# A Fourier mixing and gated convolution kernel: DFT tables laid out by quarter, odd products ahead of the halved rows, three memsets in the set-up

## The chip, the cores and the metric

The kernel runs on one core of one Trainium2 chip. The metric is the device time of one execution in microseconds (us), as a median over runs. The core's engines appear in the profile as PE (TensorE, matrix products; PEld are its weight loads), DVE (VectorE), ACT (ScalarE), POOL (GpSimd) and SP (SyncE, which here only issues DMAs). Each engine works through its own instructions in the order in which the program gives them to it; between engines, and between an engine and a DMA, the framework that builds the program puts in waits wherever two instructions touch the same data.

## What is computed

The reference, cut to what matters. The input `x` is 8 x 3136 x 256, `w_in` 256 x 1024, `conv_w` 3 x 1024, `w_out` 1024 x 256, all float32:

```python
X = np.fft.fft(x, axis=1)
X = np.fft.fft(X, axis=2)
x = X.real.astype(np.float32)

h = np.maximum(x @ w_in, 0.0)
hp = zero-padded h, one row at each end of the sequence
conv_out = sum over k of conv_w[k] * hp[:, k:k + S, :]
gate = 1.0 / (1.0 + np.exp(-conv_out))
out = (h * gate) @ w_out
```

## The kernel before

**Two stages.** For each of the 8 batches the kernel first builds the Fourier transform along the sequence as two tiles, `pt` and `qt` (`PQ[b]`), one from products with cosines and one from products with sines. Then it goes through 32 steps a batch: 4 chunks of the sequence (the chunk edges are `CUTS`) times 8 blocks of 128 of the 1024 hidden features (`f`). The transform along the features is folded into the first weight matrix: `blocks` and `column` multiply the tables `dm` with `w_in` into `G` and `ge`, once, at the start. There are 256 steps in all.

**A step** is spread over six turns of the main loop. `products` (L831, L832) makes two matrix products into PSUM tiles `pb` and `pa`, the latter on top of a `seed` (L819); `copies` (L840) brings `pb` to SBUF as `nb`; `combine` (L848) adds and subtracts them, with the clamp at zero, into the row tile `h`, forward and mirrored; `first_tap` (L854), `middle` (L858, a DMA issued on POOL that adds `h` to `g`) and `last_tap` (L863) are the convolution; `sigmoid` (L882) and `gate` (L890) follow; `mm2` multiplies with `wout` into `po`. For steps of the first chunk of a batch `row_of` (L825) has POOL zero the two cells at the ends of the row tile `h`. In turn t the loop issues, in this order: `sigmoid` and later `gate` of step t-4, `products` and `copies` of t+1, `combine` and `first_tap` of t, `seed` of t+2, `last_tap` of t-3, then `row_of` of t+1, `middle` of t, side work, and `mm2` of t-5. Side work is hung on (turn, place): in turns 0 to 10 the conversion of the remaining weights from 64-bit to 32-bit floats (`narrow`, L651 to L670), the rest of `blocks`, and in turn 0 `store`, which changes the sign of every second odd entry of the row `er` on POOL (L490, the sign change) and writes the row to memory. Later the transforms of batches 1 to 7 are spread over the turns as side work in the same way.

**The set-up** ahead of the loop is the transform of batch 0, written out by hand in the order in which each engine is to work. The sequence transform is split by parity: products with even frequencies use the table tile `tab2` (`tabs[0]`), products with odd ones `tab4` (`tabs[1]`). Partition p of a table holds sequence positions of one group; the free dimensions are `st` (cosine 0, sine 1; `tab4` has two more, mirrored, ones), the quarter `q` (`HQ` = 4 in `tab2`, two in `tab4`) and the frequency (393 or 196 columns). In `tab2` the order is st, q, frequency: all four cosine rows, then all four sine rows.

- SP loads the lower half of the columns of `tab2` (`load_even`, four DMAs) and `tab4` (`load_odd`, four DMAs); POOL issues the DMAs for the last partitions (`rest_even`, two; `rest_odd`, three).
- `mirror_even(q)` (L269, ACT, two instructions) fills the upper half of the columns of quarter q from the lower half; `mirror_tables` (L317, ACT) makes the mirrored rows of `tab4`.
- `mend_row` (L310, ACT) halves one row, the last sequence position: quarter 3 of `tab2`, cosine and sine, on partitions 96 and 97. `mend_row(1)` does the like for `tab4`.
- A `Unit` is a group of products into one PSUM tile, with `copy` (ACT) and `fin` (DVE). `odds` are the four units of the odd frequencies in the order `odd_even(1)`, `odd(1)`, `odd_even(0)`, `odd(0)`. `part(0)` gives the first two products of a unit, `part(1)` the rest. `odd` reads quarters 0 and 2 of `tab2` with a column step of two, first the cosine rows and then the sine rows; its `part(1)` reads quarter 2 and, as weights, the `parted` tiles that `scaled` (L217, ACT) makes. A `matmul` in float32 is two PE instructions.
- After `odds` come the units 4 (`feature`, which reads all columns of the cosine rows of all four quarters), 2, 3, 7 and 8, then `row_of` for the first two steps, and the loop.

In the profile `po`, `pd`, `pa`, `pb` are PSUM tiles, `as` the copies that the units make, `h` either a row tile or a `parted` tile, `raw` the 64-bit weights, `left` a scratch tile here, `er` the row of `store`. All matrix products have line L93.

Of the kernel before, what the change touches and what calls it, by code (L numbers as in the profile page):

```python
# [9 lines left out]
F32 = mybir.dt.float32  # L10
I32 = mybir.dt.int32
U32 = mybir.dt.uint32
AF = mybir.ActivationFunctionType
# [17 lines left out]
NQ = 8  # L31
# [6 lines left out]
def kernel(  # L38
# [10 lines left out]
    nc = tc.nc  # L49
    B, S, D = x.shape  # L50
    F = moe_w_in.shape[1]
    P = 128
    M = S // 2
    Q4 = S // 4
    NP = Q4 // NQ
    KR = NP + 1
    HQ = NQ // 2
    NK = M + 1
    HE = Q4 // 2 + 1
    HO = Q4 // 2  # L60
    QO = HO // 2
# [7 lines left out]
    const = ctx.enter_context(tc.tile_pool(name="const", bufs=1))  # L69
# [20 lines left out]
    act = nc.scalar.activation  # L90
# [4 lines left out]
    def spare():  # L95

        return pso.tile([P, 2, D], F32, name="po", tag="po").rearrange("p a d -> p (a d)")
# [140 lines left out]


    parted = {}  # L240
    tabs = [const.tile([P, 2, HQ, HE], F32, name="tab2"), const.tile([P, 4, 2, QO], F32, name="tab4")]
    turn = const.tile([P, 3, 2], F32, name="turn")
    rp = ctx.enter_context(tc.tile_pool(name="rp", bufs=2))
    PQ, eb, er = {}, {}, {}
# [1 line left out]

    def table(k, st, q, cols):
        if st < 2:
            return tabs[0][0:k, st, q, cols]
        return tabs[1][0:k, st - 2, q // 2, cols]  # L250

    MR = NP // 2 // 16 * 16
    assert NP == 2 * MR + 2

    HM = HO // 2 + 1

    def load_even(eng):

        for s in range(2):
            for i in range(2):  # L260
                eng.dma_start(out=tabs[0][i:2 * MR:2, s, :, 0:HM], in_=bass.AP(
                    tensor=dft_seq.tensor, offset=dft_seq.offset + (s * NQ + HQ * i) * HE,
                    ap=[[4 * NQ * HE, MR], [HE, HQ], [1, HM]]))

    def mirror_even(q):

        for st, s in enumerate(((1.0, 1.0), (-1.0, 1.0), (-1.0, -1.0), (1.0, -1.0))[q]):
            of = st if q % 2 else 1 - st
            act(tabs[0][0:KR, st, q, HM:HE][:, ::-1], tabs[0][0:KR, of, q, 0:HE - HM], AF.Copy, scale=s)  # L269

    def rest_even(eng):

        to = tabs[0].rearrange("p s q i -> p s (q i)")
        n = HQ * HE
        eng.dma_start(out=to[2 * MR:NP], in_=bass.AP(
            tensor=dft_seq.tensor, offset=dft_seq.offset + MR * 4 * NQ * HE,
            ap=[[n, 2], [NQ * HE, 2], [1, n]]))
        eng.dma_start(out=to[NP:KR], in_=bass.AP(
            tensor=dft_seq.tensor, offset=dft_seq.offset + (NP * 4 * NQ - HQ + 2) * HE,
            ap=[[n, 1], [NQ * HE, 2], [1, n]]))  # L280

    def at_(p, q, s):
        return dft_seq.offset + ((p * 4 + 2 + s) * NQ + q) * HE

    def load_odd(eng, s):

        for i in range(2):
            eng.dma_start(out=tabs[1][i:2 * MR:2, s], in_=bass.AP(
                tensor=dft_seq.tensor, offset=at_(0, HQ * i + 1, s), ap=[[4 * NQ * HE, MR], [2 * HE, 2], [1, QO]]))

    def rest_odd(eng):

        for s in range(2):
            eng.dma_start(out=tabs[1][2 * MR:NP, s], in_=bass.AP(
                tensor=dft_seq.tensor, offset=at_(MR, 1, s), ap=[[HQ * HE, 2], [2 * HE, 2], [1, QO]]))
        eng.dma_start(out=tabs[1][NP:KR, 0:2, 1], in_=bass.AP(
            tensor=dft_seq.tensor, offset=at_(NP, 1, 0), ap=[[HE, 1], [NQ * HE, 2], [1, QO]]))

    def load_turn(eng):
# [6 lines left out]

    def mend_row(par, half):

        row = tabs[0][96:NP, 0:2, HQ - 1] if par == 0 else tabs[1][96:NP, 0:2, 1]
        act(row, row, AF.Copy, scale=half[96:NP])  # L310

    def mirror_tables(h):

        k = KR if h else NP
        for to, of, s in ((2, 1, -1.0), (3, 0, 1.0)):
            for i in range(2):
                act(tabs[1][0:k, to, h, i:QO:2], tabs[1][0:k, of, h, i:QO:2], AF.Copy, scale=-s if i else s)  # L317

    class Unit:

# [391 lines left out]
    half = const.tile([P, 1], F32, name="half")  # L712
# [46 lines left out]
    begin, us, row, flip, store, odd_first, even_first = units(0)  # L759
# [6 lines left out]
    taps()  # L766
    act(turn[0:NP, 2], turn[0:NP, 1], AF.Copy, scale=-1.0)
    nc.gpsimd.memset(dm[0:1, 0, 0, 0:1], 0.0)
    nc.gpsimd.memset(tabs[1][96:KR, 0:2, 0], 0.0)
    nc.sync.dma_start(out=dm, in_=dft_dim[:, :, 0:2])  # L770
    load_odd(nc.sync, 0)
    load_odd(nc.sync, 1)
    load_even(nc.sync)
    rest_odd(nc.gpsimd)
# [39 lines left out]
    def seed(s):  # L814

        b, c, f = s
        ch, n, fs = cut(s)
        pa[s] = psa.tile([P, 512], F32, name="pa", tag="pa")
        act(pa[s][:, 0:n], eb[b, c], AF.Copy, scale=ge[:, f:f + 1])  # L819

    def row_of(s):
        hs[s] = hp.tile([P, HW], F32, name="h", tag="h")
        w = chunks[s[1]].w
        if chunks[s[1]].zeros:
            nc.gpsimd.memset(hs[s][:, 0:w:w - 1], 0.0)  # L825

    def products(s):
        b, c, f = s
        ch, n, fs = cut(s)
        pb[s] = psb.tile([P, 512], F32, name="pb", tag="pb")  # L830
        mm(pb[s][:, 0:n], G[0:P - 1, 1, fs], PQ[b][1][0:P - 1, ch.k0:ch.k1], True, True)  # L831
        mm(pa[s][:, 0:n], G[:, 0, fs], PQ[b][0][:, ch.k0:ch.k1], False, True)  # L832

    def copies(s):

        ch, n, fs = cut(s)
        p = pb.pop(s)
        nb[s] = nbp.tile([P, 2, HN], F32, name="nb", tag="nb")
        for i, cols in enumerate((ch.fcols, ch.cols)):
            act(nb[s][:, i, cols], p[:, cols], AF.Copy, scale=-1.0 if i else 1.0)  # L840

    def combine(s):

        ch, n, fs = cut(s)
        a, c = pa.pop(s), nb.pop(s)
        h = hs[s]
        for i, (to, cols) in enumerate(((h[:, ch.front], ch.fcols), (h[:, ch.back][:, ::-1], ch.cols))):
            nc.vector._custom_dve(TENSOR_ADD_SAT, out=to, in0=a[:, cols], in1=c[:, i, cols],  # L848
                                  s0=BIG, s1=0.0)

    def first_tap(s):
        n = chunks[s[1]].w - 2
        gs[s] = gp.tile([P, HW - 2], F32, name="g", tag="g")[:, 0:n]
        act(gs[s], hs[s][:, 0:n], AF.Copy, scale=cw[:, 0, s[2]:s[2] + 1])  # L854

    def middle(s):
        n = gs[s].shape[1]
        nc.gpsimd.dma_start(out=gs[s], in_=hs[s][:, 1:1 + n], accum_op=ALU.add)  # L858

    def last_tap(s):  # L860
        g, h, f, k = gs[s], hs[s], s[2], 2
        n = g.shape[1]
        stt(out=g, in0=h[:, k:k + n], scalar=cw[:, k, f:f + 1], in1=g, op0=ALU.mult, op1=ALU.add)  # L863
# [14 lines left out]
    def sigmoid(s):  # L878

        v, p, r = shares(s)  # L880
        for c in [slice(0, r.stop)] if whole(s) else (slice(p.start, r.stop), v):
            act(gs[s][:, c], gs[s][:, c], AF.Sigmoid, scale=cw[:, 1, s[2]:s[2] + 1])  # L882
# [13 lines left out]
    def keep(s):  # L896

        b, c, f = s
        r = shares(s)[2]
        if r.start < r.stop:  # L900
            nc.scalar.copy(out=left[:, f, b % 2 * LEFT:(b % 2 + 1) * LEFT], in_=gs[s][:, r])
# [37 lines left out]
    odds = [us[j] for j in (0, 1, 5, 6)]  # L939
# [28 lines left out]
        u.part(0)  # L968
    for u in odds[::2]:
        u.part(1)  # L970
    odds[0].copy()
    odds[0].fin()
    mend_row(0, half)
    odds[1].part(1)
    odds[1].copy()
    odds[1].fin()
    mirror_even(1)
    odds[2].copy()
    odds[2].fin()
    mirror_even(3)  # L980
    odds[3].part(1)
    odds[3].copy()
    odds[3].fin()
    exponent()
    mantissa()

    n = chunks[0].k1
    for i, u in enumerate(us[j] for j in (4, 2, 3, 7, 8)):
        u.matmuls(0, 1)
        if i == 1:  # L990
            p = spare()
# [10 lines left out]
            lower()  # L1002
    steps = [(b, c, f) for b in range(B) for c in range(len(chunks)) for f in range(NF)]
    per = len(chunks) * NF
    for i in range(2):
        row_of(steps[i])
    side = {}
    taken = set()
# [45 lines left out]
    for b in range(1, B):  # L1054
# [4 lines left out]
        n = per * b - (2 if b == 1 else 3) - c0  # L1059
        at(max(c0, per * (b - 1) + 1), "pe", begin)  # L1060
        cs = [c0 + i * n // len(us) for i in range(len(us) + 1)]
        for i, u in enumerate(us):
            k = cs[i + 1] - cs[i]
# [8 lines left out]
    for b in range(1, B):  # L1072
        ops, singles, pres = fold_ops(b)
        c0, n = ends[b - 1], ends[b] - ends[b - 1]
# [4 lines left out]
        else:  # L1079
            if b == 2:  # L1080
                c0, n = c0 + 3, n - 3
# [16 lines left out]
    n = len(steps)  # L1098
# [6 lines left out]
    for t in range(n + LAG):  # L1105
        def run(where):
            for fn in side.get((t, where), []):
                fn()
        if 0 <= t - 4 < n:
            sigmoid(steps[t - 4])  # L1110
        if t + 1 < n:
            products(steps[t + 1])
            copies(steps[t + 1])
        run("first")
        run("act")
        if t >= LAG:
            keep(steps[t - LAG])
        if t < n:
            combine(steps[t])
        if t + 2 < n:  # L1120
            seed(steps[t + 2])
        if t < n:
            first_tap(steps[t])

        run("dve")
        if 0 <= t - 3 < n:
            last_tap(steps[t - 3])
        if 0 <= t - 4 < n:
            gate(steps[t - 4])
        if 1 <= t < n - 1:  # L1130
            row_of(steps[t + 1])
        if t < n:
            middle(steps[t])
        run("pool")
        run("load")
        if t >= LAG:
            mm2(steps[t - LAG])
        run("pe")
# [66 lines left out]
```

## Time and profile before

| | us |
|---|---|
| median of 3 runs | 1158.92 |
| lowest and highest run | 1158.70, 1159.15 |
| profiled execution | 1159.72 |
| its span, first to last instruction | 1157.9 |
| PE, DVE, ACT, POOL busy in it | 1137.4, 960.3, 901.4, 376.3 |

The granted TensorE clock is at full speed throughout. Times in the profile are microseconds from the start of the span. A timeline row has start, duration, engine and line, operation, the tile written, the tiles read, their shapes, how many instructions were merged into the row (x4), and in brackets the idle time of the engine before the row and what ended it. Instructions of one engine overlap at their ends, so the next may start before the recorded end of the one before. A row of the waits says who waited for what, with total, number and longest. A row of the stretches has the stretch, its length, and the busy time of PE, PEld, DVE, ACT and POOL, each with its count of instructions, then clock, DMA share and GB/s.

### The profile page before, as it was taken

Reading aid. Unit: us, or ns where it says so; the run is one execution under the profiler, and the core shown is the slowest. Engines: PE = TensorE matmul, PEld = TensorE weight load, DVE = VectorE, ACT = ScalarE, POOL = GpSimd, SP = SyncE. Lnnn points to the kernel's source line nnn. Section 1 sums busy time; section 2 is a strip of 40 time slices with the busy share of each in tenths; the row PEclk is TensorE's granted clock in tenths of the full one; section 3 lists DMA queues with packets and bytes.
Section 4 is the critical chain, followed back from the end, with each engine's and each line's share of the span. In section 5 each row is a group of like instructions: output and inputs, shape, how many; then the busy total and the mean of one; then the engine's idle time right before and its main releaser. Section 6 shows DMA issues by size and latency. Waiting matters only on the chain.

```text
span 1157.9 us, 15068 instructions
## 1 busy us (share of the span) xinstructions
PE 1137.4 (98%) x4824; PEld 887.7 (77%) x4824; DVE 960.3 (83%) x1452; ACT 901.4 (78%) x1707; POOL 376.3 (32%) x484
## 2 busy tenths in 40 slices
PE   6999999999999999999999999999999999999998
PEld 4667787788777777778777777777778777777777
DVE  8899899988988989798878878888886767877775
ACT  3788868877787778787878778887877777888884
POOL 6425523642343242425132332422212222222223
PEclk9999999999999999999999999999999999999999
DMA  9787975876767586756676666765664656666664
GB/s 246 172 118 167 180 168 117 182 166 143 172 127 162 118 192 153 166 119 151 139 173 133 152 142 123 175 129 119 138 132 90 128 117 137 139 132 128 123 118 101
DMA packets 107595, 167.49 MB, mean 145 GB/s; under 512 B 32104, under 2 KB 62838, under 8 KB 107517
## 3 DMA queue, kind: packets, MB, share of 16 engines
q0 software_dynamic: 42160, 115.87, 51.9%
q1 hardware_dynamic: 64616, 50.53, 15.9%
q8 instruction: 38, 0.62, 0.2%
q10 hardware_dynamic: 741, 0.14, 0.1%
q14 instruction: 40, 0.33, 0.1%
HBM read 37.80 MB, written 25.74 MB: 55 GB/s over the span
## 4 chain that ended last, share of the span: by engine, by line
PE 85%; DVE 5%; ACT 5%; issue 2%; POOL 2%; DMA 1%; SPq 0%; ACTq 0%; POOLq 0%; DVEq 0%
PE po L93 53%; PE pb L93 13%; PE pa L93 13%; PE pd L93 6%; DVE g L863 1%; DVE g L890 1%; ACT os L918 1%; ACT nb L840 1%; POOL xh L129 1%; DMA xh<-in_x_dram 1%; DVE h L848 1%; ACT pa L819 1%; ACT g L882 0%; ACT g L854 0%; DMA tab<-dft_seq_dram 0%
## 5 line engine op out<-in xcount | busy, mean ns | idle before, releaser
L93 PE MATMUL po<-wout,g 128*128 128x256 f32 x3072 | 706.4, 379 | 3.8 <-DVE g L890 3.7
L93 PEld LDWEIGHTS po<-wout,g 128*128 128x128 f32 x3072 | 580.5, 190 | 149.0 <-DVE g L890 18.2
L858 POOL DMA_DIRECT2D g<-h x256 | 220.0, 859 | 729.3 <-ACT g L854 459.9
L840 ACT ACTIVATE nb<-pb 128x386 f32<-128x386 f32 (+3 forms) x512 | 227.5, 499 | 168.0 <-PE pb L93 167.1
L848 DVE CUSTOM_DVE_ANT_0 h<-pa,nb 128x386 f32<-128x386 f32 (+3 forms) x512 | 265.2, 559 | 34.8 <-PE pa L93 22.6
L882 ACT ACTIVATE g<-g,cw 128x770 f32<-128x770 f32 (+3 forms) x264 | 246.0, 935 | 46.3 <-DVE g L863 44.9
L863 DVE SCALAR_TENSOR_TENSOR g<-h,cw,g 128x770 f32<-128x770 f32 (+1 forms) x256 | 265.6, 1038 | 0.3 <-DMA g<-h 0.3
L890 DVE TENSOR_TENSOR g<-g,h 128x770 f32<-128x770 f32 (+1 forms) x248 | 240.3, 969 | 22.3 <-ACT g L882 22.1
L854 ACT ACTIVATE g<-h,cw 128x770 f32<-128x770 f32 (+1 forms) x256 | 244.1, 953 | 0.0
L93 PE MATMUL pb<-qt,G 127*128 127x387 f32 (+2 forms) x512 | 213.7, 498 | 1.5 <-ACT nb L840 1.1
L93 PE MATMUL pa<-pt,G 128*128 128x387 f32 (+2 forms) x512 | 212.1, 495 | 0.8 <-ACT pa L819 0.7
L819 ACT ACTIVATE pa<-eb,ge 128x387 f32<-128x387 f32 (+2 forms) x256 | 155.3, 607 | 2.1 <-DVE h L848 0.3
L93 PEld LDWEIGHTS pa<-pt,G 128*128 128x128 f32 x512 | 96.6, 189 | 75.6 <-issue 18.5
L129 POOL DMA_INDIRECT xh<-in_x_dram,idx x64 | 98.4, 1538 | 20.2 <-issue 12.7
L93 PE MATMUL pd<-tab,w 98*128 98x197 f32 (+2 forms) x448 | 97.6, 317 | 0.0
L93 PEld LDWEIGHTS pb<-qt,G 127*128 127x128 f32 x512 | 90.9, 190 | 8.5 <-ACT nb L840 2.9
L93 PEld LDWEIGHTS pd<-tab,w 98*128 98x128 f32 (+1 forms) x448 | 82.0, 191 | 8.9
L918 ACT COPY os<-po 128x256 f32<-128x256 f32 x196 | 57.4, 393 | 6.3 <-PE po L93 6.3
L398 DVE TENSOR_TENSOR as<-as,pd 128x196 f32<-128x196 f32 x14 | 5.0, 358 | 46.0 <-ACT as L394 46.0
L176 POOL COPY w<-xh 98x4 f32<-98x4 f32 (+1 forms) x30 | 37.5, 1251 | 7.9 <-DVE xh L170 7.9
L154 DVE TENSOR_TENSOR xh<-xh 98x1020 f32<-98x1020 f32 (+1 forms) x32 | 38.7, 1211 | 0.5 <-DMA xh<-in_x_dram,idx 0.5
L165 DVE TENSOR_TENSOR xh<-xh 98x1024 f32<-98x1024 f32 (+1 forms) x32 | 38.9, 1216 | 0.1
(150 smaller groups left out, 430.9 us busy)
## 6 DMA issues: line engine op xcount, KB each, us to landing
g<-h POOLq DMA_DIRECT2D x192, 385.0 KB, 3.9
g<-h POOLq DMA_DIRECT2D x64, 416.0 KB, 4.3
out_dram<-os SPq DMA_DIRECT2D x96, 256.0 KB
xh<-in_x_dram SPq DMA_DIRECT2D x16, 784.0 KB
eb<-ed SPq DMA_DIRECT2D x16, 193.5 KB
raw<-in_moe_w_in_dram SPq DMA_DIRECT2D x4, 512.0 KB
raw<-in_moe_w_out_dram SPq DMA_DIRECT2D x1, 2048.0 KB
eb<-ed SPq DMA_DIRECT2D x8, 209.0 KB
```

Source lines behind the costliest of these rows:

```text
L93: nc.tensor.matmul(o, l, r, start=start, stop=stop, skip_group_check=True)
L129: nc.gpsimd.indirect_dma_start(out=xh[b, h][0:NP, 7 - m].rearrange("p q d -> p (q d)"), out_offset=None, in_=bass.AP(tensor=x.tensor, offs ...
L165: vt(flat(to, to + 2), flat(0, 2), flat(2, 4), op=op)
L819: act(pa[s][:, 0:n], eb[b, c], AF.Copy, scale=ge[:, f:f + 1])
L840: act(nb[s][:, i, cols], p[:, cols], AF.Copy, scale=-1.0 if i else 1.0)
L848: nc.vector._custom_dve(TENSOR_ADD_SAT, out=to, in0=a[:, cols], in1=c[:, i, cols], s0=BIG, s1=0.0)
L854: act(gs[s], hs[s][:, 0:n], AF.Copy, scale=cw[:, 0, s[2]:s[2] + 1])
L858: nc.gpsimd.dma_start(out=gs[s], in_=hs[s][:, 1:1 + n], accum_op=ALU.add)
L863: stt(out=g, in0=h[:, k:k + n], scalar=cw[:, k, f:f + 1], in1=g, op0=ALU.mult, op1=ALU.add)
L882: act(gs[s][:, c], gs[s][:, c], AF.Sigmoid, scale=cw[:, 1, s[2]:s[2] + 1])
L890: vt(g, g, h[:, 0:r.stop], op=ALU.mult)
L918: nc.scalar.copy(out=osb[:, j % 2], in_=pt[:, j % 2])
```

## The change

Three things are done. The tables are laid out with the quarter outside and cosine and sine beside each other inside it; every access is rewritten to match, `rest_even` becomes four DMAs in place of two, and `mend_row(0)` halves only the lower half of the columns, which `mirror_even(3)` then copies to the upper half. In the set-up, `part(1)` of both `odd` units now comes ahead of every `copy` and `fin` of the odd units, and so ahead of `mend_row(0)`; `mirror_even(1)` and `mirror_even(3)` both follow the second unit's `fin`, where `mirror_even(3)` had followed the third's. And `row_of` is called for three steps ahead of the loop instead of two, so the loop begins its own calls one turn later.

```diff
-    tabs = [const.tile([P, 2, HQ, HE], F32, name="tab2"), const.tile([P, 4, 2, QO], F32, name="tab4")]
+    tabs = [const.tile([P, HQ, 2, HE], F32, name="tab2"), const.tile([P, 2, 4, QO], F32, name="tab4")]
...
-                eng.dma_start(out=tabs[0][i:2 * MR:2, s, :, 0:HM], in_=bass.AP(
+                eng.dma_start(out=tabs[0][i:2 * MR:2, :, s, 0:HM], in_=bass.AP(
...
-            act(tabs[0][0:KR, st, q, HM:HE][:, ::-1], tabs[0][0:KR, of, q, 0:HE - HM], AF.Copy, scale=s)
+            act(tabs[0][0:KR, q, st, HM:HE][:, ::-1], tabs[0][0:KR, q, of, 0:HE - HM], AF.Copy, scale=s)
 
     def rest_even(eng):
 
-        to = tabs[0].rearrange("p s q i -> p s (q i)")
         n = HQ * HE
-        eng.dma_start(out=to[2 * MR:NP], in_=bass.AP(
-            tensor=dft_seq.tensor, offset=dft_seq.offset + MR * 4 * NQ * HE,
-            ap=[[n, 2], [NQ * HE, 2], [1, n]]))
-        eng.dma_start(out=to[NP:KR], in_=bass.AP(
-            tensor=dft_seq.tensor, offset=dft_seq.offset + (NP * 4 * NQ - HQ + 2) * HE,
-            ap=[[n, 1], [NQ * HE, 2], [1, n]]))
+        for s in range(2):
+            eng.dma_start(out=tabs[0][2 * MR:NP, :, s], in_=bass.AP(
+                tensor=dft_seq.tensor, offset=dft_seq.offset + (MR * 4 + s) * NQ * HE,
+                ap=[[n, 2], [HE, HQ], [1, HE]]))
+            eng.dma_start(out=tabs[0][NP:KR, :, s], in_=bass.AP(
+                tensor=dft_seq.tensor, offset=dft_seq.offset + ((NP * 4 + s) * NQ - HQ + 2) * HE,
+                ap=[[n, 1], [HE, HQ], [1, HE]]))
...
-            eng.dma_start(out=tabs[1][i:2 * MR:2, s], in_=bass.AP(
+            eng.dma_start(out=tabs[1][i:2 * MR:2, :, s], in_=bass.AP(
...
-        row = tabs[0][96:NP, 0:2, HQ - 1] if par == 0 else tabs[1][96:NP, 0:2, 1]
+        row = tabs[0][96:NP, HQ - 1, :, 0:HM] if par == 0 else tabs[1][96:NP, 1, 0:2]
         act(row, row, AF.Copy, scale=half[96:NP])
...
     for u in odds[::2]:
         u.part(1)
-    odds[0].copy()
-    odds[0].fin()
-    mend_row(0, half)
-    odds[1].part(1)
-    odds[1].copy()
-    odds[1].fin()
-    mirror_even(1)
-    odds[2].copy()
-    odds[2].fin()
-    mirror_even(3)
-    odds[3].part(1)
-    odds[3].copy()
-    odds[3].fin()
+    for u in odds[1::2]:
+        u.part(1)
+    for i, u in enumerate(odds):
+        u.copy()
+        u.fin()
+        if i == 0:
+            mend_row(0, half)
+        if i == 1:
+            mirror_even(1)
+            mirror_even(3)
     exponent()
     mantissa()
...
-    for i in range(2):
+    for i in range(3):
         row_of(steps[i])
...
-        if 1 <= t < n - 1:
+        if 2 <= t < n - 1:
             row_of(steps[t + 1])
```

More of the change, by code (lines that the diff above doesn't have):

```diff
@@ L248, in table @@
         if st < 2:
-            return tabs[0][0:k, st, q, cols]
-        return tabs[1][0:k, st - 2, q // 2, cols]
+            return tabs[0][0:k, q, st, cols]
+        return tabs[1][0:k, q // 2, st - 2, cols]
     MR = NP // 2 // 16 * 16
@@ L293, in rest_odd @@
         for s in range(2):
-            eng.dma_start(out=tabs[1][2 * MR:NP, s], in_=bass.AP(
+            eng.dma_start(out=tabs[1][2 * MR:NP, :, s], in_=bass.AP(
                 tensor=dft_seq.tensor, offset=at_(MR, 1, s), ap=[[HQ * HE, 2], [2 * HE, 2], [1, QO]]))
-        eng.dma_start(out=tabs[1][NP:KR, 0:2, 1], in_=bass.AP(
+        eng.dma_start(out=tabs[1][NP:KR, 1, 0:2], in_=bass.AP(
             tensor=dft_seq.tensor, offset=at_(NP, 1, 0), ap=[[HE, 1], [NQ * HE, 2], [1, QO]]))
@@ L316, in mirror_tables @@
             for i in range(2):
-                act(tabs[1][0:k, to, h, i:QO:2], tabs[1][0:k, of, h, i:QO:2], AF.Copy, scale=-s if i else s)
+                act(tabs[1][0:k, h, to, i:QO:2], tabs[1][0:k, h, of, i:QO:2], AF.Copy, scale=-s if i else s)
     class Unit:
@@ L768 @@
     nc.gpsimd.memset(dm[0:1, 0, 0, 0:1], 0.0)
-    nc.gpsimd.memset(tabs[1][96:KR, 0:2, 0], 0.0)
+    nc.gpsimd.memset(tabs[1][96:KR, 0, 0:2], 0.0)
     nc.sync.dma_start(out=dm, in_=dft_dim[:, :, 0:2])
```

## The prediction

> **What bounds the kernel now.** I read the page's busy shares first, then busy time by stretch, then who waited for whom on TensorE and VectorE, then the timeline of the two places where a wait stood out.
>
> ```profile
> PE 1137.4 (98%) x4824; PEld 887.7 (77%) x4824; DVE 960.3 (83%) x1452; ACT 901.4 (78%) x1707; POOL 376.3 (32%) x484
> ```
>
> ```profile
> 104.00:1130.00 1026.00, 1023.55 (x4335) 803.79 (x4335) 850.08 (x1272) 816.71 (x1507) 317.09 (x400) 1.00 0.68 142
> ```
>
> From 104 to 1130 us TensorE (first of the busy columns) idles 1026.00 - 1023.55 = 2.45 us. Its work there does not change, so whatever brings it to 104 us earlier shortens the kernel by as much, and nothing else in the diff can. The question is the first 104 us.
>
> ```profile
> PE po L93 <- DVE g L890: 1.6, 2, 1.1
> ...
> PE po L93 <- ACT tab L310: 0.9, 1, 0.9
> ```
>
> ```profile
> DVE h L848 <- POOL h L825: 2.2, 1, 2.2
> ```
>
> The first view is TensorE from 20 to 130 us, the second VectorE from 20 to 110 us (total, times, longest). The diff touches the writers behind the last two rows: the halved rows (`mend_row`, L310) and the memset of `row_of` (L825).
>
> **The order of the set-up.** The stall on L310, with ScalarE (ACT) beside TensorE (PE); one float32 product is two PE instructions:
>
> ```profile
> 26.41 1.69 ACT L217 ACTIVATE h<-w,turn 98x256 f32<-98x256 f32 x4
> ...
> 27.60 0.86 PE L93 MATMUL po<-tab,h 98*128 98x197 f32 x4
> ...
> 28.33 0.94 ACT L310 ACTIVATE tab<-tab,half 2x786 f32<-2x786 f32 x1
> ...
> 29.33 2.37 PE L93 MATMUL po<-tab,h 98*128 98x197 f32 x12 [0.87 <-ACT tab L310]
> ...
> 30.34 0.33 ACT L417 COPY as<-po 128x197 f32<-128x197 f32 x1 [1.06 <-PE po L93]
> 30.68 0.62 ACT L269 ACTIVATE tab<-tab 99x196 f32<-99x196 f32 x2
> ...
> 31.21 0.30 ACT L394 COPY as<-po 128x196 f32<-128x196 f32 x1
> ...
> 31.42 0.62 ACT L269 ACTIVATE tab<-tab 99x196 f32<-99x196 f32 x2
> ...
> 31.85 0.48 PEld L93 LDWEIGHTS pd<-tab,ea 99*1 99x1 f32 x16 [0.47 <-issue]
> ```
>
> `odd(1).part(1)` has four products. The first two (the x4) use the cosine of quarter 2 and ran; the other two use the sine of quarter 2 and stood until L310 ended, though L310 touches only quarter 3, cosine and sine. In the old layout the sine of quarter 2 lies between those two rows, so the wait fits an order by the span of addresses rather than by elements. Laid out by quarter, the two rows of quarter 3 are neighbours with nothing between; and in the new program the products come ahead of `mend_row`. Either removes the stall.
>
> What it is worth: the 12 instructions start (2.37 - 0.34)/11 = 0.185 us apart (0.34 being one instruction's length, from the x4: 0.86 = length + 3 x 0.17 to 0.185). Without the wait the fifth would start at 27.60 + 4 x 0.185 = 28.34, not 29.33: 0.99 us. Their operand is ready: the four L217 end at 28.10.
>
> What is late next is ScalarE, since the feature products (PEld 31.85) read the table that the last L269 pair, `mirror_even(3)`, completes. Old: the pair starts at 31.42, its first half ends about 0.36 later (0.62 for two that overlap), and PEld follows at 31.85; by its own pitch TensorE could have gone at 29.33 + 12 x 0.185 = 31.55. New: L417 starts 0.99 earlier, at 29.35. The halved rows are done by then: they shrink from 786 to 394 elements a partition, which cost
>
> ```profile
> 23.05 0.62 ACT L310 ACTIVATE tab<-tab,half 2x392 f32<-2x392 f32 x1
> ```
>
> so L310 runs 28.33 to 28.95, and its saved 0.32 us falls into ScalarE's wait for L417. Both L269 pairs now follow directly and the L394 between them moves behind (31.42 - 31.21 = 0.21): the last pair starts at 31.42 - 0.99 - 0.21 = 30.22 and PEld goes at 30.65. That is **1.20 us**. If the feature products waited instead for the last odd product to end (29.33 + 2.37 = 31.70), it is 0.99. I take 1.2, because PEld's 31.85 follows ScalarE's 31.78 more closely. What hangs behind moves along: VectorE's fins wait on L417, the delayed L394 is needed only after four VectorE operations, and the second `odd(0).copy` waits on those. The cover for the later L394 is thus VectorE's queue; gone, it would cost 0.5.
>
> **The layout.** The loads of halves keep their number and sizes. `rest_even` goes from two POOL issues to four, and the rows around them are:
>
> ```profile
> 16.76 0.58 POOL L275 DMA_DIRECT2D tab<-dft_seq_dram  x1
> ...
> 17.31 0.55 POOL L278 DMA_DIRECT2D tab<-dft_seq_dram  x1
> ...
> 17.98 2.56 SPq L261 DMA_DIRECT2D tab<-dft_seq_dram  x4
> ...
> 19.18 0.71 POOL L176 COPY w<-xh 98x4 f32<-98x4 f32 x1 [1.17 <-DVE xh L170]
> ...
> 24.35 0.62 ACT L269 ACTIVATE tab<-tab 99x196 f32<-99x196 f32 x2 [0.69 <-DMA tab<-dft_seq_dram]
> ```
>
> Two more at 0.55 to 0.58 are 1.13 us, inside the 1.17 us that POOL idles before L176; without that cover POOL's copies would move by as much, and their reader, an even product, comes only after the feature products of 31.85. The reader of the table (24.35) waits for DMA; the last of the old loads is SP's, issued at 17.98 + 2.56 - 0.61 = 19.93, the last new POOL issue at about 18.45. I price the layout at 0; its upper bound is a rival below.
>
> **The third memset.** VectorE, POOL and ScalarE around the stall:
>
> ```profile
> 46.81 0.71 DVE L667 SCALAR_TENSOR_TENSOR raw<-raw,left 128x512 f32<-128x512 uint32 x1
> 49.70 1.02 DVE L848 CUSTOM_DVE_ANT_0 h<-pa,nb 128x385 f32<-128x385 f32 x2 [2.19 <-POOL h L825]
> 50.65 0.68 DVE L661 SCALAR_TENSOR_TENSOR win<-raw,win 128x512 int32<-128x512 int32 x1
> 51.36 0.69 DVE L670 SCALAR_TENSOR_TENSOR win<-raw,win 128x512 f32<-128x512 f32 x1
> 51.97 0.42 DVE L651 TENSOR_SCALAR wout<-raw 128x512 int32<-128x512 int32 x1
> 52.31 1.02 DVE L848 CUSTOM_DVE_ANT_0 h<-pa,nb 128x385 f32<-128x385 f32 x2
> ...
> 55.24 1.02 DVE L848 CUSTOM_DVE_ANT_0 h<-pa,nb 128x385 f32<-128x385 f32 x2
> ```
>
> ```profile
> 47.67 1.98 POOL L490 TENSOR_SCALAR er<-er 1x392 f32<-1x392 f32 x1
> 49.52 0.14 POOL L825 MEMSET h<- 128x2 f32 x1
> ...
> 53.30 0.57 POOL L825 MEMSET h<- 128x2 f32 x1
> ```
>
> ```profile
> 50.24 0.87 ACT L840 ACTIVATE nb<-pb 128x385 f32<-128x385 f32 x2 [0.29 <-PE pb L93]
> ```
>
> The sign change (L490) holds POOL until 49.65, the memset for step 2 stands behind it, and `combine` (L848) waits 2.19 us. With the memset done in the set-up, where POOL otherwise idles, L848 starts at 49.70 - 2.19 = 47.51. Not all 2.19 is kept. L848 of step 3 needs the copies that ScalarE starts at 50.24 (0.87 for two halves, the first done near 50.7), and L848 of step 4 the memset of step 4, which stays behind an accumulating DMA at 53.30 and ends at 53.87. The former bound leaves 1.5 us of step 3, the latter 55.24 - 53.9 = 1.3 of step 4: at most 1.3 survive. Below, the part is worth 0 if other work then waits there, which is rival (b).
>
> And VectorE now works while L490 runs. Elsewhere this looks so:
>
> ```profile
> 35.91 0.55 POOL L459 TENSOR_TENSOR er<-h 1x196 f32<-1x196 f32 x1
> ...
> 36.91 0.68 DVE L667 SCALAR_TENSOR_TENSOR raw<-raw,left 128x512 f32<-128x512 uint32 x1
> 36.97 1.10 POOL L459 TENSOR_TENSOR er<-h 1x196 f32<-1x196 f32 x1
> ```
>
> The same POOL operation takes 0.55 us, but 1.10 when it starts beside an L667 that reads two SBUF operands, and ends 0.48 after it: it waited. L490 would be running when the first such operation, L661, comes at 47.51 + 0.95 = 48.46; then it is VectorE that waits, to 49.65. L661 at 49.65 instead of 50.65 is **1.0 us**; with the 0.71, 0.61 and 0.34 by which the starts of L661, L670, L651 and L848 lie apart, step 3 starts at 51.31, behind its copies.
>
> The Trainium skill ("SBUF — State Buffer", "Who interferes with whom") states this as a lock: a VectorE instruction with two SBUF inputs and a GpSimd instruction that reads SBUF exclude each other, whoever comes first keeping the port. The two L459 rows agree (0.55 against 1.10). Without the lock the part would be worth 1.3, with it 1.0.
>
> Does 1.0 reach TensorE?
>
> ```profile
> ACT g L882 <- DVE g L863: 5.2, 6, 1.6
> ```
>
> ```profile
> 81.21 2.86 PE L93 MATMUL po<-wout,g 128*128 128x256 f32 x12 [1.10 <-DVE g L890]
> ```
>
> ScalarE waits six times for VectorE's last tap, 0.9 us in the mean, and TensorE at 81.21 for 1.10 us: VectorE sets the pace, and the wait is longer than the gain. After it TensorE runs on, so the whole 1.0 passes.
>
> **Sum.** 1.2 + 1.0 + 0 = 2.2 us. The profiled execution took 1159.72 us (span 1157.9): changed, 1157.5 and 1155.7. It lies 0.8 above the median of the runs, 1158.92, which becomes **1156.7**.
>
> **The rivals.** (a) No port wait: 2.5 us, 1156.4. For it: nothing shows L661 itself held. (b) The memset's gain does not arrive, since TensorE from 58 to 80 us has its own pace: then 1.2 us, 1157.7. Against it stands the wait at 81.21. (c) The change does not do what it says: the order is not by span, and the moved `mend_row` now waits for the products ahead of it. They end about 28.34 + 2.37 = 30.71, L310 ends 31.4, L417 (30.34) goes to 31.45 and the feature products to 32.7, 0.85 later than before; with the memset's 1.0 it is 1158.8. Against: the first two products read a row just below the span and did not wait. (d) Slower: if order is by span, cosine and sine loads, contiguous blocks before, now interlace, and the sine's issue on SP would stand until the cosine's landed. A landing costs
>
> ```profile
> 19.93 4.31 DMA tab<-dft_seq_dram
> ```
>
> 4.3 us; the reader at 24.35 has no slack worth naming (TensorE's x12 needs L217's end, 28.10, by 28.34), so about 4.1 is lost and 2.2 won: 1160.8. If the odd tables wait likewise, 1165. It decides from a wait of 2.4 us on. Against: ACT's column writes run beside VectorE's writes to neighbouring columns of the same tile:
>
> ```profile
> 14.70 0.69 DVE L191 TENSOR_TENSOR w<-xh 98x508 f32<-98x508 f32 x1
> 14.70 0.20 ACT L196 COPY w<-xh 98x4 f32<-98x4 f32 x1 [2.96 <-DVE xh L165]
> ```
>
> so equal strides seem told apart exactly, and only unequal ones (a step of two in the product, one in L310) by span.
>
> **How the numbers follow.** The forecast 0.48, (a) 0.22, (b) 0.12, (c) 0.07, (d) 0.11. The forecast's own range is 1156.3 to 1157.2. The 8-in-10 range runs from 1155.8, a little under (a) for chip-to-chip scatter, to 1159.0, which takes in (b) and (c). 0.2% is 2.3 us, about what a measurement of this kernel tells from no change: 1156.6 divides faster from same. Of the forecast 0.4 lies below it (0.19), of (a) nearly all (0.21): faster 0.40. Slower by 0.2% (over 1161.2) are the dearer half of (d) and what I have overlooked: 0.11. Same: 0.49.
>
> **What would show it.** Right: no TensorE wait for L310; the last instruction of the odd products starts about 30.4; PEld of the feature near 30.65; no VectorE wait for L825; an L661 of about 1.8 us (blocked) ending with L490; TensorE's wait of about 1 us at 81.21 still there, some 2.2 us earlier. Wrong: a gap between SP's L261 issues, L269 starting after 24.4, L310 starting after 30.7, or a new VectorE wait ahead of 62 us that eats the 1.0.

## The result, and the profile after

The changed kernel takes 1156.84 us (median of 20 runs, 1156.06 to 1157.44) where the kernel before takes 1159.28 us beside it. The ratio is 0.9978, with a 95% interval of 0.9971 to 0.9985: 2.4 us less. The profiled execution took 1157.24 us with a span of 1155.5, and the span before was 1157.9.

Busy time by stretch of the changed kernel, the stretch of steady work set 2 us earlier than before's (stretch, its length, then PE, PEld, DVE, ACT and POOL busy):

```profile
102.00:1128.00 1026.00, 1023.56 (x4335) 803.76 (x4335) 850.17 (x1273) 816.82 (x1505) 318.77 (x399) 1.00 0.68 142
```

PE's idle time there is 2.44 us, against 2.45 before. So the gain was made ahead of that stretch and carried to the end. Who waited for whom after the change, first PE from 20 to 110 us, then DVE:

```profile
PE po L93 <- DVE g L890: 1.1, 1, 1.1
PE pb L93 <- ACT nb L840: 1.1, 2, 0.7
PE pa L93 <- ACT pa L819: 0.7, 2, 0.4
PE pb L93 <- ACT G L792: 0.5, 1, 0.5
PE po L93 <- ACT tab L269: 0.4, 1, 0.4
```

```profile
DVE h L848 <- PE pa L93: 0.8, 1, 0.8
DVE g L890 <- ACT g L882: 0.5, 1, 0.5
```

Both waits that the change aimed at are gone, PE's for L310 and DVE's of 2.2 us for L825. In their place stands a wait of DVE of 0.8 us for a product. PE's short wait for the table's first mirrored half (L269) comes from the loads of this execution; when the changed kernel ran again, it was absent. The set-up in the timeline:

```profile
24.53 0.62 ACT L269 ACTIVATE tab<-tab 99x196 f32<-99x196 f32 x2 [0.95 <-DMA tab<-dft_seq_dram]
...
27.79 2.96 PE L93 MATMUL po<-tab,h 98*128 98x197 f32 x16
...
28.51 0.62 ACT L310 ACTIVATE tab<-tab,half 2x394 f32<-2x394 f32 x1
...
29.39 0.33 ACT L417 COPY as<-po 128x197 f32<-128x197 f32 x1 [0.26 <-PE po L93]
29.74 1.14 ACT L269 ACTIVATE tab<-tab 99x196 f32<-99x196 f32 x4
...
30.72 0.87 PE L93 MATMUL pd<-tab,ea 99*1 99x197 f32 x16
```

The sixteen parted products run in one piece, L310 takes 0.62 us beside them, and the feature products start at 30.72 instead of 31.88. The table's loads happened to land 0.18 us later in this execution (L269 at 24.53 against 24.35), so the comparison is taken from the first parted product to the feature products: 30.72 - 27.79 = 2.93 us, before 31.88 - 27.60 = 4.28, the 31.88 from this row of before:

```profile
31.88 0.88 PE L93 MATMUL pd<-tab,ea 99*1 99x197 f32 x16 [0.18 <-issue]
```

The second place, DVE (`combine` of steps 1 to 4, with L661 between) and then POOL:

```profile
44.25 1.02 DVE L848 CUSTOM_DVE_ANT_0 h<-pa,nb 128x385 f32<-128x385 f32 x2
...
46.25 1.02 DVE L848 CUSTOM_DVE_ANT_0 h<-pa,nb 128x385 f32<-128x385 f32 x2
47.19 0.76 DVE L661 SCALAR_TENSOR_TENSOR win<-raw,win 128x512 int32<-128x512 int32 x1
...
49.85 1.03 DVE L848 CUSTOM_DVE_ANT_0 h<-pa,nb 128x385 f32<-128x385 f32 x2 [0.84 <-PE pa L93]
...
52.78 1.02 DVE L848 CUSTOM_DVE_ANT_0 h<-pa,nb 128x385 f32<-128x385 f32 x2
```

```profile
46.49 2.00 POOL L490 TENSOR_SCALAR er<-er 1x392 f32<-1x392 f32 x1
48.49 0.90 POOL L858 DMA_DIRECT2D g<-h  x1
49.13 0.38 POOL L825 MEMSET h<- 128x2 f32 x1
```

`combine` of step 2 no longer waits, and L661 runs in 0.76 us in the middle of the sign change. `combine` of step 4 starts at 52.78 instead of 55.24, 2.46 us earlier. At the point where DVE sets TensorE's pace this is still there:

```profile
78.78 2.86 PE L93 MATMUL po<-wout,g 128*128 128x256 f32 x12 [1.10 <-DVE g L890]
```

81.21 - 78.78 = 2.43 us, the same as the 2.4 us at the end.

### The profile page after: what moved, and what is told of

Same layout as the page of the kernel before. It is cut to its first block, busy times and chain, and to the rows that moved or that the text cites. A ratio compares the mean times of both kernels' runs of the same rounds, so it can differ in the third digit from the quotient of the medians.

```text
span 1155.5 us, 15071 instructions
## 1 busy us (share of the span) xinstructions
PE 1135.8 (98%) x4824; PEld 887.5 (77%) x4824; DVE 960.7 (83%) x1452; ACT 901.0 (78%) x1707; POOL 377.9 (33%) x486
## 4 chain that ended last, share of the span: by engine, by line
PE 86%; DVE 5%; ACT 4%; issue 2%; DMA 1%; POOL 1%; SPq 0%; ACTq 0%; DVEq 0%; POOLq 0%
PE po L93 54%; PE pb L93 13%; PE pa L93 13%; PE pd L93 6%; DVE g L863 1%; DVE g L890 1%; ACT os L918 1%; ACT nb L840 1%; DMA xh<-in_x_dram 1%; DVE h L848 1%; POOL xh L129 1%; ACT g L882 0%; ACT pa L819 0%; DMA tab<-dft_seq_dram 0%; ACT g L854 0%
## 5 line engine op out<-in xcount | busy, mean ns | idle before, releaser
L176 POOL COPY w<-xh 98x4 f32<-98x4 f32 (+1 forms) x30 | 37.3, 1244 | 6.7 <-DVE xh L170 6.7
```

## The experiments

**The layout alone.** The changed kernel's tables, loads and halved rows, with the old order of the odd units and two memsets.

```diff
+    tabs = [const.tile([P, HQ, 2, HE], F32, name="tab2"), const.tile([P, 2, 4, QO], F32, name="tab4")]
+        row = tabs[0][96:NP, HQ - 1, :, 0:HM] if par == 0 else tabs[1][96:NP, 1, 0:2]
```

> The layout by quarter alone, with the old order of the set-up and two memsets. Theory (waits follow the span of addresses that an access covers, so the sine row of quarter 2 lay inside the halved rows' span): TensorE no longer waits for L310, the fifth of the parted products starts near 28.3 to 28.5 instead of 29.33, the feature products near 30.9 to 31.1 instead of 31.88, and the kernel takes about 1.0 us less; VectorE's wait of 2.2 us for L825 stays. Rival (the wait has another cause, such as the order of the instructions alone): the wait of 0.87 us for L310 stays and the time is that of before. Second question: the first L269 started 0.18 us later in the changed kernel (24.53 against 24.35). If the layout's loads do it, it is near 24.5 here too, and near 24.35 in the kernels with the old layout; if it is scatter, it follows neither.

1158.39 us beside 1159.15, ratio 0.9992 (0.9983 to 1.0001). PE's wait for L310 is gone, and the feature products follow the first parted product by 30.72 - 27.57 = 3.15 us, 1.13 less than before:

```profile
27.57 2.96 PE L93 MATMUL po<-tab,h 98*128 98x197 f32 x16
...
30.72 0.87 PE L93 MATMUL pd<-tab,ea 99*1 99x197 f32 x16 [0.19 <-issue]
```

The timing agrees with that but cannot tell it from nothing by itself. The trace can: the layout removes the stall, with the order untouched. The new order adds 3.15 - 2.93 = 0.22 us, through the copy that no longer stands between the two mirrors.

**The order alone.** Odd products ahead of the halved rows, in the old layout. It ran twice.

```diff
-    odds[0].copy()
-    odds[0].fin()
-    mend_row(0, half)
-    odds[1].part(1)
...
+    for u in odds[1::2]:
+        u.part(1)
+    for i, u in enumerate(odds):
+        u.copy()
+        u.fin()
+        if i == 0:
+            mend_row(0, half)
```

> The new order alone, with the old layout and two memsets. Theory of the span: the halved rows' write now comes after the products in the program and covers the sine row of quarter 2, so L310 waits until the last parted product has ended, near 30.8 instead of starting at 28.33; the copy L417 behind it moves to about 31.7 from 30.34, the feature products to about 33.0 from 31.88, and the kernel takes about 1.1 us more than before. Rival (accesses are told apart by elements, or the order alone removes the stall): L310 starts near 28.3, the feature products near 30.7, and the kernel takes about 1.2 us less.

> The order alone once more, beside the next kernel. Theory (TensorE's gap of 2.33 us lets the clock gate fall to half for some 7 us, in most executions but not all, since it depends on where the gap falls): executions near 1160.8 us at a mean clock of 1.000 and others at 1163 to 1168 with 0.993 to 0.996. Rival (the low clock was a disturbance of the first time): all near 1160.8 at 1.000.

1165.70 us, ratio 1.0048 (1.0032 to 1.0064), and 1165.83, ratio 1.0042 (1.0024 to 1.0060): slower by far more than expected. The mechanism is as expected. L310 stands 2.39 us for the products and PE then stands for ACT:

```profile
26.87 2.96 PE L93 MATMUL po<-tab,h 98*128 98x197 f32 x16
...
29.87 0.94 ACT L310 ACTIVATE tab<-tab,half 2x786 f32<-2x786 f32 x1 [2.39 <-PE po L93]
...
32.17 0.87 PE L93 MATMUL pd<-tab,ea 99*1 99x197 f32 x16 [2.33 <-issue]
```

From the first parted to the feature products it is 5.30 us, 1.02 more than before, where 1.1 was expected. The rest is the clock. Busy time by stretch of the same execution, of the first run (PEclk is the third number from the end):

```profile
30.00:32.00 2.00, 0.00 (x0) 0.00 (x0) 0.77 (x3) 1.95 (x6) 1.70 (x2) 1.00 1.05 390
32.00:34.00 2.00, 1.83 (x21) 1.37 (x22) 1.98 (x6) 1.55 (x7) 1.44 (x2) 0.79 1.08 318
34.00:36.00 2.00, 2.00 (x11) 2.00 (x10) 1.98 (x4) 0.79 (x3) 1.93 (x3) 0.50 1.01 246
...
38.00:40.00 2.00, 2.00 (x11) 2.00 (x10) 1.59 (x3) 0.00 (x0) 0.00 (x0) 0.50 0.96 144
40.00:42.00 2.00, 2.00 (x16) 2.00 (x16) 0.64 (x3) 1.93 (x5) 0.00 (x0) 1.00 0.44 66
```

After the gap the granted clock falls to half until 40 us, about 7 us, in the middle of a chain of products. The profile of the second run, which took 1166.49 us against 1163.14, has the same gap (2.34 us, to 32.50), and there the clock stays down until about 47 us, twice as long:

```profile
42.00:44.00 2.00, 2.00 (x7) 2.00 (x7) 0.63 (x2) 1.31 (x3) 0.00 (x0) 0.50 0.01 0
44.00:48.00 4.00, 4.00 (x9) 2.24 (x9) 3.29 (x7) 0.87 (x2) 0.00 (x0) 0.59 0.00 0
```

It does not always happen: of the 15 executions of the two runs, ten had a mean clock of 0.992 to 0.996 and took 1163.14 to 1167.98 us, five had 0.998 to 1.000 and took 1160.69 to 1161.67.

**The order alone, with the gap filled.** Two idle products after the last odd product; they write a bank that nobody reads.

```diff
     for u in odds[1::2]:
-        u.part(1)
+        u.part(1); keep_on(u is odds[3] and 2)
```

> The order alone, with two idle products (about 2 us of TensorE time, into a bank nobody reads) between the last odd product and the feature products, so that L310 still waits but TensorE has no gap. Theory: L310 and the feature products as late as in the order alone (near 29.9 and 32.2), but the granted clock stays at 1.000 in all executions and the time is about 1160.8 us, 1.6 above before. Rival (the clock falls for another reason, such as the narrow feature products): it falls here too and the time scatters up to 1168.

1160.45 us beside 1159.37, ratio 1.0010 (1.0001 to 1.0018), all eleven executions between 1160.07 and 1161.38 at a mean clock of 0.999 or 1.000. L310 still waits 2.42 us, PE idles 0.61 ahead of the feature products, and the clock stays up (timeline, then a stretch):

```profile
29.99 0.94 ACT L310 ACTIVATE tab<-tab,half 2x786 f32<-2x786 f32 x1 [2.42 <-PE po L93]
...
32.29 0.88 PE L93 MATMUL pd<-tab,ea 99*1 99x197 f32 x16 [0.61 <-issue]
```

```profile
34.00:36.00 2.00, 2.00 (x15) 2.00 (x14) 1.97 (x5) 0.91 (x3) 1.80 (x3) 1.00 0.96 255
```

So the order alone costs 1.1 us by its wait (1160.45 against 1159.37), and up to 7.5 us more (1167.98) by the gap that the wait leaves in PE's work.

**The halving split in two.** Old layout, old order, two memsets; the cosine row and the sine row of quarter 3 are halved by an instruction each.

```diff
-        row = tabs[0][96:NP, 0:2, HQ - 1] if par == 0 else tabs[1][96:NP, 0:2, 1]
-        act(row, row, AF.Copy, scale=half[96:NP])
+        for row in [tabs[0][96:NP, s, HQ - 1] for s in range(2)] if par == 0 else [tabs[1][96:NP, 0:2, 1]]:
+            act(row, row, AF.Copy, scale=half[96:NP])
```

> Old layout, old order, two memsets; only the halving of quarter 3 is given as two instructions, the cosine row and the sine row, so that no access spans the sine row of quarter 2. Theory of the span: the wait for L310 goes although nothing else has moved; the fifth parted product starts near 28.34, the feature products near 30.9, and the kernel takes about 1.0 us less, as with the layout alone. Rival (the stall hangs on something else that layout or order change): the wait stays, now of about the same 0.9 us, and the time is that of before.

```profile
27.49 2.96 PE L93 MATMUL po<-tab,h 98*128 98x197 f32 x16
...
28.15 1.13 ACT L310 ACTIVATE tab<-tab,half 2x393 f32<-2x393 f32 x2
...
30.85 0.88 PE L93 MATMUL pd<-tab,ea 99*1 99x197 f32 x16 [0.40 <-issue]
```

The stall is gone although neither layout nor order has moved, and the feature products follow after 3.36 us, 0.92 less than before. The time, 1158.82 us with a ratio of 0.9994 (0.9985 to 1.0003), is too coarse to show it. The trace settles the cause: what PE waited for was the span of the one instruction, not its place. Whether the products' column step has a part in it, as the prediction has it, was not tested.

**Three memsets alone.** Old layout and order.

```diff
-    for i in range(2):
+    for i in range(3):
         row_of(steps[i])
...
-        if 1 <= t < n - 1:
+        if 2 <= t < n - 1:
```

> Three memsets alone, old layout and order. Theory from the changed kernel's trace (L661 is not held by POOL's sign change, and L848 of step 3 waits for TensorE's pa product instead): VectorE's wait of 2.19 us for L825 is gone, a wait of about 0.8 us stands ahead of L848 of step 3, L661 takes 0.7 to 0.8 us, step 4's L848 starts 1.2 to 1.3 us earlier than 55.24, and the kernel takes about 1.25 us less. Rival (the prediction's): L661 is held for about 1 us, ends with the sign change, and the gain is 1.0 us. The wait of 0.87 us for L310 stays in both.

1158.13 us, ratio 0.9988 (0.9979 to 0.9997): 1.0 us in the medians, which cannot tell the prediction's 1.0 from the expectation's 1.25. The trace can. DVE in that kernel:

```profile
44.86 1.02 DVE L848 CUSTOM_DVE_ANT_0 h<-pa,nb 128x385 f32<-128x385 f32 x2
...
47.79 0.78 DVE L661 SCALAR_TENSOR_TENSOR win<-raw,win 128x512 int32<-128x512 int32 x1
...
50.46 1.03 DVE L848 CUSTOM_DVE_ANT_0 h<-pa,nb 128x385 f32<-128x385 f32 x2 [0.82 <-PE pa L93]
...
53.39 1.02 DVE L848 CUSTOM_DVE_ANT_0 h<-pa,nb 128x385 f32<-128x385 f32 x2
```

From `combine` of step 1 to that of step 4 it is 53.39 - 44.86 = 8.53 us. Before it was 55.24 less step 1's start, which this row of before gives, 9.82:

```profile
45.42 1.02 DVE L848 CUSTOM_DVE_ANT_0 h<-pa,nb 128x385 f32<-128x385 f32 x2
```

So 1.29 us of the 2.19 are kept. The changed kernel has 52.78 - 44.25 = 8.53 too. The gain reaches TensorE: the row that stood at 81.21 is at 79.40, 1.81 us earlier, of which 0.56 were there at step 1 already, and 1.25 are new.

```profile
79.40 2.86 PE L93 MATMUL po<-wout,g 128*128 128x256 f32 x12 [1.10 <-DVE g L890]
```

One part of the expectation missed. The wait for L310 is still there, but with 0.47 us, and the feature products follow the first parted product by 31.32 - 27.44 = 3.88 us where before had 4.28:

```profile
28.77 2.37 PE L93 MATMUL po<-tab,h 98*128 98x197 f32 x12 [0.47 <-ACT tab L310]
```

Layout and order of the set-up are those of before. The loads came earlier here (the first L269 at 23.78 against 24.35), and with them L310 by 0.56 us (27.77 against 28.33), but PE's parted products only by 0.16. So the length of the stall is that of an execution and not a constant of the kernel.

**Who holds whom.** The changed kernel with the sign change as a product of two SBUF operands.

```diff
-            nc.gpsimd.tensor_scalar(out=er[b][:, 3:NK:4], in0=er[b][:, 3:NK:4], scalar1=-1.0, scalar2=None, op0=ALU.mult)
+    minus = const.tile([1, HO // 8], F32, name="minus")
+    nc.gpsimd.memset(minus, -1.0)
...
+            v = er[b][:, 3:NK:4].rearrange("p (a i) -> p a i", a=8)
+            gt(v, v, minus[:, 0:HO // 8].unsqueeze(1).to_broadcast([1, 8, HO // 8]), op=ALU.mult)
```

> The changed kernel with the sign change as a product of two SBUF operands on POOL (tensor_tensor with a short row of -1) in place of an operation with one operand. Theory (VectorE's operation with two SBUF inputs is held only by a POOL operation that itself reads two operands at once): L661 is held until the sign change ends, so it takes 1.2 us or more instead of 0.76, and step 4's L848 may come later by up to 0.3 us. Rival (neither holds the other there): L661 stays at 0.7 to 0.8 us.

A single execution, 1157.13 us. DVE, then POOL:

```profile
46.87 1.06 DVE L661 SCALAR_TENSOR_TENSOR win<-raw,win 128x512 int32<-128x512 int32 x1
```

```profile
46.17 1.22 POOL L490 TENSOR_TENSOR er<-er,minus 1x392 f32<-1x392 f32 x1
```

L661 is 0.38 us longer than its usual 0.68 and now is held. The 1.2 us of the expectation was too much, since this form of the sign change is itself done in 1.22 us instead of 2.00, at 47.39: from there to L661's end, 47.93, is 0.54. The hold costs nothing here: step 3's wait shrinks from 0.84 to 0.51, and step 4 still follows step 1 by 52.48 - 43.94 = 8.54 us. The changed kernel itself has a second case, POOL's L459 with two operands and DVE's L667, which takes 1.04 instead of 0.69 and also ends 0.54 after it:

```profile
35.84 0.54 POOL L459 TENSOR_TENSOR er<-h 1x196 f32<-1x196 f32 x1
```

```profile
35.88 1.04 DVE L667 SCALAR_TENSOR_TENSOR raw<-raw,left 128x512 f32<-128x512 uint32 x1
```

In both cases a POOL operation with two operands, running first, held back a DVE operation that reads two SBUF operands. The sign change with a single operand, on the same cells, did not, and was itself held by at most 0.05 us: it took 2.00 to 2.02 us in the five kernels that have L661 beside it, and 1.97 or 1.98 in the six others. That the number of operands decides is not shown, because the kind of instruction changed with it. In the other direction it does not decide. L176, a POOL copy with one operand, takes about 0.5 us in eleven of its thirty cases in the kernel before, those with no DVE operation on two SBUF operands beside it. In the nineteen others it takes 0.59 to 3.30 us and ends 0.03 to 0.05 us behind such an operation, as here:

```profile
98.77 2.14 POOL L176 COPY w<-xh 98x4 f32<-98x4 f32 x1
```

```profile
99.89 0.96 DVE L890 TENSOR_TENSOR g<-g,h 128x770 f32<-128x770 f32 x1
```

**The next wait.** The changed kernel with the third block of folded weights one turn later, so that step 3's `pa` product, for which DVE now waits, comes first.

```diff
-        at((0, 0, 1, 3)[i], "pe", lambda i=i: blocks(i))
+        at((0, 0, 2, 3)[i], ("first", "pe")[i - 2], lambda i=i: blocks(i))
```

> The changed kernel with the third block of the folded weights (blocks(2) and its column) issued one turn later, between products and seed of turn 2, so that TensorE makes step 3's pa product ahead of it. Theory (with the memset out of the way, VectorE's 0.84 us wait ahead of step 3's L848 is for that product and ScalarE's copies): the wait shrinks to 0.6 us or less, since the copies, POOL's memset of step 3 (ends 49.5) and ScalarE's own queue come next; gain 0 to 0.4 us. Rival (that wait sets the rest): the full 0.8 us is won.

1157.79 us against 1156.72 of the changed kernel beside it: a loss of 1.1 us where 0 to 0.4 were to be won.

```profile
49.58 1.02 DVE L848 CUSTOM_DVE_ANT_0 h<-pa,nb 128x385 f32<-128x385 f32 x2 [0.54 <-POOL h L825]
...
53.83 1.02 DVE L848 CUSTOM_DVE_ANT_0 h<-pa,nb 128x385 f32<-128x385 f32 x2 [1.23 <-POOL h L825]
```

Step 3's wait shrinks to 0.54 and is for POOL's memset again. But the evictions of the block now stand in ACT's queue ahead of step 2's first tap; the accumulating DMA on POOL waits for that tap, and step 4's memset behind it, so step 4 waits 1.23 us. In the changed kernel the same DMA waits for the same tap, but step 4's memset is done at 52.54, 0.24 us before DVE comes to step 4.

**Another way to the same.** Old layout, halving split in two and cut to the lower half of the columns, new order, three memsets; and the changed kernel once more beside it.

> The old layout with the halving of quarter 3 split in two instructions (lower half of the columns, as in the change), the new order and three memsets. Theory (the layout's only use is to take the sine row out of the span): the same as the changed kernel within 0.3 us; L310 starts without a wait although it follows the products, TensorE has no gap, the clock stays at full speed. Rival (the layout does something more): about 1 us or more above the changed kernel, or L310 waiting for the products as in the order alone. If the old layout's loads come earlier, it may be 0.2 to 0.5 us faster than the changed kernel.

> The changed kernel once more, beside the next ones. Both theories: about 0.9978 of the kernel before. It is also a second look at when the first L269 starts (24.53 in the first look, 23.78 to 24.35 in the kernels with the old layout): within that spread if the late start was scatter of the loads, again at 24.5 or later if the layout's loads cause it.

1156.80 us, ratio 0.9976 (0.9967 to 0.9986), and 1156.72, ratio 0.9978 (0.9969 to 0.9987): the same. In both the feature products follow the first parted product by 2.93 us. It does not beat the changed kernel, and none of the kernels tried does.

The starts of the first L269 are 24.53, 24.32, 24.08, 24.22 and 24.01 in the five kernels laid out by quarter, 24.23 in the mean, and 24.35, 23.53, 23.78, 24.16, 24.15, 23.79 and 23.62 in the seven others, 23.91 in the mean. The ranges overlap. Whether the layout's loads cost some tenths is not settled; a cost of a microsecond is excluded, since the two kernels above differ by 0.1 us.

## Why the prediction was right, and where it was not

**The set-up** was to give 1.2 us, 0.99 from the stall and 0.21 from the copy. From the first parted product it gave 4.28 - 2.93 = 1.35, of which the layout alone has 1.13 and the order 0.22. So the stall was priced too low. The products start 0.175 us apart ((2.96 - 0.34)/15 over the sixteen) and not 0.185; at that pitch the twelve behind the stall would have taken 2.27 us and not 2.37, so about 0.1 us of what was read as their pitch belongs to the stall. That gives 29.33 - 28.30 + 0.10 = 1.13 us, as the layout alone had it; this is worked out, not tested. And the size holds for the profiled pair: against the 3.88 us of the three memsets alone, the same subtraction gives 0.95.

The reading behind it, that the wait follows the span of addresses, is shown by the two opposite experiments: the split halving loses the stall in the old place, and the order alone, in the old layout, gains a wait of the other direction. That is the wait that rival (c) feared, L310 standing for the products, but it comes because the order is by span and not, as (c) had it, because it isn't. In the changed kernel the layout avoids it. The sentence "either removes the stall" was half wrong: the order takes it from PE and gives it to ACT.

**The layout** at 0 stands to within some tenths. POOL's cover was used up as counted: L176 starts at 19.21 without an idle row, where it had been 19.18.

```profile
18.58 0.55 POOL L278 DMA_DIRECT2D tab<-dft_seq_dram  x1
...
19.21 0.70 POOL L176 COPY w<-xh 98x4 f32<-98x4 f32 x1
```

Rival (d), cosine and sine loads waiting for each other, did not come: SP issues its four L261 in 2.55 us without a gap, before in 2.56.

```profile
18.17 2.55 SPq L261 DMA_DIRECT2D tab<-dft_seq_dram  x4
```

The spans of these loads do interlace now, so span alone does not make a wait. Why they are told apart, by their equal steps as the prediction argued or because one queue issues them, is not shown. One of the signs against the prediction did appear, an L269 after 24.4 (24.53). It was no gap between the loads that made it, and the same kernel later had 24.08.

**The memset** was to give 1.0 and gave 1.29. The step that failed is "then it is VectorE that waits, to 49.65": L661 was not held by the sign change (0.76 us, and 0.78 with the memsets alone). Rival (a) came true instead. The Trainium skill ("SBUF — State Buffer", "Who interferes with whom") speaks of any GpSimd instruction that reads SBUF. For the sign change the measurement differs, and it decides. The hold was inferred from two L459 rows, where a POOL operation of another kind, with two operands, was held by DVE; the sign change has one operand and was to hold DVE. In its form with two operands it does, by 0.38 us. What in the form with one lets L661 pass stays open, since the copy L176 has one operand, too, and is held.

Two bounds on that part were read too loosely. Step 3's `combine` was bounded by ACT's copies near 50.7, which was said to leave 1.5 us (52.31 less 50.7 is 1.6), but it waits for PE's `pa` product (0.82 to 0.84 us), which the prediction did not list. And step 4's memset, given as the limit at 1.3 us, is done 0.24 us before DVE comes to step 4 from its own queue. It did not set the 1.29: of the 0.90 us lost, step 3's wait takes 0.84, and that the number agrees with 1.3 is luck. The experiment with the later block shows the memset deciding as soon as ACT is later.

**The way to TensorE** held: the wait of 1.10 us at 78.78 is still there, and all that DVE had won passed. The two parts make 1.35 + 1.29 = 2.64 us; less the 0.18 by which this execution's loads were late it is 2.46, as at `combine` of step 4, and 2.43 at 78.78. The predicted sum, 2.2 us, was short in both terms and stands against 2.4 measured. That 1156.7 comes so near to 1156.84 us is luck in part: the prediction started from 1158.92, and the kernel before took 1159.28 beside the changed one.

## What to carry to other kernels

Read a wait against the exact rows that both instructions touch: where they share none, as here, look at the order of the tile's dimensions and at accesses with a hole, because splitting one instruction into two can do the work of a new layout. Moving work ahead of a write can bring the same conflict back as a wait of the writer, as long as the write's span covers what the work reads. And a small cell-clearing operation in a queue behind a long one is worth issuing early, but count what the freed engine meets next: of 2.19 us, 1.29 remained. And take a hold between two engines from a row with the same instructions in the same roles, or give it as a range.

## What was not expected of the hardware

A gap of 2.33 us in PE's work halved the granted clock (0.50 in the rows above) for about 7 us in one profiled execution and, at 2.34 us, for about 14 in the other, and lowered the mean clock in ten of fifteen executions. Filled with idle products down to 0.61 us, it did so in none of eleven. The stall of 0.87 us in the kernel before left the clock at 1.00. The Trainium skill ("TensorE: Matmul & The Clock Gate", "What's actually happening") describes a gate that looks at windows of some 3.4 us which run freely, and ("Why this matters for your kernels") advises against gaps over about 3 us. The scatter from execution to execution fits windows that run freely; the length does not, as 2.33 us was enough here.

The sign change, an operation of one operand on one partition, took POOL longer than the form with two operands on the same cells: 1.97 to 2.02 us against 1.22.
